# Moving one more product in six units to GpSimd, one more mask to ScalarE, and turning the weights later in a fused top-k attention and mixture-of-experts kernel

## Chip, core and metric

The kernel runs on one core of a Trainium2 chip. The metric is device time in microseconds (us) of one execution. The kernel before takes 995.38 us, the median of three runs (995.27 to 997.89). The engines are written as in the profile: PE is TensorE, PEld its weight loads, DVE is VectorE, ACT is ScalarE, POOL is GpSimd, and SP is the queue that issues the transfers.

## What is computed

There are two stages. The first is attention over 8 batches, 8 heads, 576 positions and head size 64, in which every row keeps only its 32 largest scores. The second routes the 4608 resulting rows of 512 to 8 experts, each of which takes at most 80 rows.

```python
def _attn_ref(q, k, v):
    scores = scale * np.matmul(q, k.transpose(0, 1, 3, 2))
    kth = np.partition(scores, -top_k, axis=-1)[..., -top_k:-top_k + 1]     # top_k = 32
    mask = scores >= kth
    scores = np.where(mask, scores, -1000000000.0)
    scores = scores - np.max(scores, axis=-1, keepdims=True)
    attn = np.exp(scores)
    attn = attn / (np.sum(attn, axis=-1, keepdims=True) + 1e-09)
    return np.matmul(attn, v).astype(np.float32)

def _moe_ref(x, w_gate, w1, w2, capacity):       # capacity = 80
    logits = x @ w_gate
    expert_idx = np.argmax(logits, axis=1)
    # ... softmax over the 8 logits; gate_w is that of the expert chosen
    out = np.zeros((N, D), dtype=np.float32)
    for e in range(E):
        # ... tok_idx: rows of expert e, cut to the 80 largest gate_w
        h = np.maximum(x[tok_idx] @ w1[e], 0.0)
        out[tok_idx] = gate_w[tok_idx, None] * (h @ w2[e])
    return out
```

## The kernel before

The attention works on one pair of heads at a time. There are 32 pairs. A pair has five tiles of rows: four full ones of 128 rows of each of the two heads, and a last one with the remaining 64 rows of both heads. A "unit" is 128 rows with their 576 scores, so a full tile has two units, the last tile has one, a pair has nine, and the kernel has 288.

All engines are programmed by hand as a pipeline. In each step, one unit enters. Its search for the 32nd largest score runs over five steps, interleaved on VectorE with the searches of earlier units. The letters in the strings below are the pieces of that search. "G" is one of six maxima over 96 scores. "a" to "e" are the top-8 maxima and replacements among the 48 candidates, and "e" also starts ScalarE's sign of the scores against the 24th largest, whose sum counts them. "y" is the product of scores and signs, "g" the top-8 of that product, "h" the pick of the threshold, and "m" the mask of the scores below it. "z" is a reciprocal.

```python
def search(self, i):
    ...                                     # "a" to "e": maxima and replacements on VectorE
            nc.scalar.activation(sign, s, Act.Sign, bias=w9[:, 7:8], scale=-1.0, accum_out=cnt)
    ...
    y = self.rows.tile([P, S], F32, name="y", tag="y", bufs=1)
    engine = nc.gpsimd if i in self.odd else nc.vector
    engine.tensor_tensor(out=y, in0=s, in1=sign, op=Alu.mult)                      # "y"
    yield
    nc.vector.max(out=w9[:, 8:], in_=y)                                            # "g"
    yield
    ...
    nc.vector.scalar_tensor_tensor(out=pick, in0=past, scalar=cnt, in1=w9[:, 7:],
                                   accum_out=self.thr[:, i : i + 1], ...)          # "h"

def below(self, i):                                                                # "m"
    self.mask[i] = self.rows.tile([P, S], BF16, name="mask", tag="mask", bufs=3)
    if i in self.odd:
        nc.scalar.activation(self.mask[i], self.s[i], Act.Relu, bias=self.thr[:, i : i + 1], scale=-1.0)
        return
    nc.gpsimd.tensor_scalar(self.mask[i], self.s[i], self.thr[:, i : i + 1], None, op0=Alu.is_lt)
```

`self.odd` holds every second unit. Those have the product on GpSimd and the mask on ScalarE; the others have the product on VectorE and the mask on GpSimd.

When both units of a tile have their masks, TensorE turns the scores so that keys lie on partitions. The turned mask, times a large negative number, is accumulated on top, and ScalarE takes the exponential out of PSUM. Each head's 576 keys are cut into five chunks of 128, the last of which overlaps the fourth, so a full tile has ten chunks.

```python
def turn_w(self, n, t):
    ...
    for h in range(g):                       # scores: 5 chunks of each head
        for c in range(NK):
            nc.tensor.matmul(dst[h][c], lhsT=sc[:, keys[c]], rhs=ident, ..., is_transpose=True)
    for h in range(g):                       # masks: the same chunks
        for c in (NF, *range(NF)):
            nc.tensor.matmul(dst[h][c], lhsT=mk[:, keys[c]], rhs=huge if i + h in self.odd else minus, ...)
    nc.scalar.activation(wT[:, 2 * NF : 2 * NF + g, :]..., cc[:, : g * P], Act.Exp, ...)     # last chunks
    nc.scalar.activation(wT[:, : g * NF, :], ab..., Act.Exp, ...)                            # the other eight
```

The rest of a step, in program order, where `i` is the step:

```python
for c in "ghmGbGycGdGGGeaz" if i % 2 else "GbGhmgcGdGeGGyaz":   # y of unit i-2, g of i-3, h and m of i-4
    ...
if rest: back()                              # weights times values, unit i-5 (the last tile of a pair)
if whole(i - 4): self.turn_w(*units[i - 4][:2])
for u in done: self.divide(*u)               # ScalarE: xn = weighted sum / sum of weights
if busy: self.front(*units[f][:2])           # scores of a tile that enters four steps on; ScalarE: s
if not rest: back()
if due and not busy: self.turn(due.pop())    # q and k of the next pair turned; ScalarE: both
for g in list(later): ...                    # norm: xn turned, ScalarE: xT; then gate logits, ScalarE: part
```

`front`, `turn`, and the two parts of `norm` all use one PSUM buffer, `sp`, of four banks. So each of them on TensorE waits until ScalarE has emptied the one before. The turned weights have one buffer `ab` of their own.

After the attention, `finish` routes the rows and computes the experts. Weights of experts 0 to 3 are loaded during the attention, those of expert 4 when the attention's memory is released, and the others into buffers that earlier experts leave.

Of the kernel before, what the change touches and what calls it, by code (L numbers as in the profile page):

```python
# [22 lines left out]
HUGE = 2.0 ** 100  # L23
# [4 lines left out]
def kernel(  # L28
# [120 lines left out]
    class Attention:  # L149


        def __init__(self, stack, lean):
            self.lean = lean
            pool = lambda name, bufs, **kw: stack.enter_context(tc.tile_pool(name=name, bufs=bufs, **kw))
            self.nat, self.qkp, self.rows = pool("nat", 1), pool("qkp", 2), pool("rows", 2)
            self.small, vpool = pool("small", 4), pool("vpool", 1)
            self.ps_s, self.ps_w, self.ps_c = (pool(n, k, space=PSUM) for n, k in (("ps_s", 1), ("ps_w", 1), ("ps_c", 2)))
            self.qk, self.turned, self.lg = {}, {}, {}
            self.s, self.top, self.cnt, self.y, self.mask, self.w, self.xn = ({} for _ in range(7))
            self.thr, self.z = thr_all, z_all  # L160
            self.odd = set()


            self.vb = []
            for j in range(1 if lean else 3):
                t = vpool.tile([P, NK, 2, D + 1], F32, name=f"vb{j}")
                nc.gpsimd.memset(t[:, :, :, D : D + 1], 1.0)
                nc.gpsimd.memset(t[: P - TL, NF, :, :], 0.0)
                self.vb.append(t)

            self.xT = vpool.tile([P, NK * P], F32, name="xT")
            nc.gpsimd.memset(self.xT[:, S:], 0.0)

        def load(self, n, b, hp):
            one = bass.ds(b, 1)
            tiles = []
            for name, src in (("qn", q), ("kn", k)):
# [7 lines left out]
                tiles.append(t)  # L185
            t = self.vb[n % len(self.vb)]
            for h in range(2):
                nc.sync.dma_start(
                    t[:, :NF, h, :D], v[one, 2 * hp + h, : NF * P, :].rearrange("o (c p) d -> p (o c) d", p=P))
            nc.sync.dma_start(  # L190
                t[P - TL :, NF, :, :D], v[one, 2 * hp : 2 * hp + 2, NF * P :, :].rearrange("o h p d -> p (o h) d"))
            self.qk[n] = tiles
# [23 lines left out]
        def front(self, n, t):  # L216
# [11 lines left out]
            s = self.rows.tile([P, 2 * S], F32, name="s", tag="s", bufs=2 if self.lean else 5)  # L228
# [43 lines left out]

        def below(self, i):

            self.top.pop(i)
            self.mask[i] = self.rows.tile([P, S], BF16, name="mask", tag="mask", bufs=3)
            if i in self.odd:
                nc.scalar.activation(self.mask[i], self.s[i], Act.Relu, bias=self.thr[:, i : i + 1], scale=-1.0)  # L278
                return
            nc.gpsimd.tensor_scalar(self.mask[i], self.s[i], self.thr[:, i : i + 1], None, op0=Alu.is_lt)  # L280
# [13 lines left out]
        def drop(self, i):  # L294

            s, top = self.s[i], self.top.pop(i)
            self.mask[i] = self.rows.tile([P, S], BF16, name="mask", tag="mask", bufs=2)
            nc.vector.tensor_scalar(self.mask[i], s, self.thr[:, i : i + 1], top[:, 0, 0:1], op0=Alu.is_lt, op1=Alu.add)

        def turn_w(self, n, t):  # L300
# [9 lines left out]
            keys = [slice(c * P, c * P + P) for c in range(NF)] + [slice(S - P, S)]  # L310
            dst = [[ab[:, h, c, :] for c in range(NF)] + [cc[:, h * P : (h + 1) * P]] for h in range(g)]

            for h in range(g):
                sc = self.s.pop(i + h)
                for c in range(NK):
                    nc.tensor.matmul(dst[h][c], lhsT=sc[:, keys[c]], rhs=ident, start=c == 0 or (c == NF and h == 0), stop=False,  # L316
                                     is_transpose=True, skip_group_check=True)
            for h in range(g):
                mk = self.mask.pop(i + h)
                for c in (NF, *range(NF)):  # L320
                    nc.tensor.matmul(dst[h][c], lhsT=mk[:, keys[c]], rhs=huge if i + h in self.odd else minus, start=False, stop=True, skip_group_check=True)  # L321
            wT = self.rows.tile([P, 2 * NK, P], F32, name="wT", tag="wT")
            nc.scalar.activation(wT[:, 2 * NF : 2 * NF + g, :].rearrange("p h r -> p (h r)"), cc[:, : g * P], Act.Exp,  # L323
                                 scale=scale / TINY)
# [3 lines left out]
        def back(self, n, t):  # L328
# [3 lines left out]
            for h in range(2 if t < NF else 1):  # L332
                o = slice(2 * P + h * (D + 1), 2 * P + (h + 1) * (D + 1))
                for c in range(NK):
                    for r in range(0, P, TL):
                        nc.tensor.matmul(cc[r : r + TL, o], lhsT=wT[:, h * NF + c if c < NF else 2 * NF + h, r : r + TL],  # L336
                                         rhs=vb[:, c, h if t < NF else r // TL, :], start=(c == 0), stop=(c == NF))
            self.w[n, t] = cc

        def over(self, n, t):  # L340
# [3 lines left out]
            sums = self.w[n, t][:, 2 * P : 2 * P + 2 * (D + 1)].rearrange("p (h d) -> p h d", h=2)[:, :g, D]  # L344
# [5 lines left out]
        def divide(self, n, t):  # L350
# [3 lines left out]
            for h in range(2):  # L354
                if t < NF:
                    p, o, j, m = slice(0, P), 2 * P + h * (D + 1), h, P
                else:
                    p, o, j, m = slice(TL * h, TL * h + TL), 2 * P, 0, TL
                nc.scalar.activation(self.xn[n][:m, t, h, :], cc[p, o : o + D], Act.Copy, scale=self.z[p, n % NP, t, j : j + 1])  # L359

        def norm(self, n, b, hp, bi, nb, cs=range(NK)):
# [15 lines left out]
            yield 1  # L377
# [50 lines left out]
        def run(self, slow):  # L428
# [6 lines left out]
            self.odd = set(range(1, NU, 2))  # L435
# [10 lines left out]
            def step(i, last):  # L446
                if 0 <= i < NU:
                    n, t, h = units[i]
                    if t == 2 and h == 1 and n + 2 < NP:
                        self.load(n + 2, *divmod(n + 2, HP))  # L450
                    if t in (1, 3) and h == 0 and slow and n:
# [5 lines left out]
                back = dict(a=0, b=1, c=1, d=1, e=1, y=2, g=3, h=4, m=4)  # L457

                for c in "ghmGbGycGdGGGeaz" if i % 2 else "GbGhmgcGdGeGGyaz":
# [11 lines left out]
                    elif c == "m":  # L471
                        if 0 <= i - back[c] < NU:
                            self.below(i - back[c])
                    elif i - back[c] in second:
                        next(second[i - back[c]])
# [3 lines left out]
                def back():  # L479
                    if whole(i - 5):  # L480
                        self.back(*units[i - 5][:2])
                        drawn.append(units[i - 5][:2])


                rest = whole(i - 4) and units[i - 4][2] == 2
                if rest:
                    back()
                if whole(i - 4):
                    self.turn_w(*units[i - 4][:2])
# [15 lines left out]
                for g in list(later):  # L505
                    if ready[g] and busy and not last:
# [10 lines left out]
            with tc.manual_schedule():  # L517
                self.load(0, 0, 0)
                self.load(1, *divmod(1, HP))
# [3 lines left out]
                while i < NU + 6 or later:  # L523
                    step(i, i >= NU + 5)
# [3 lines left out]
        def batch(self, b):  # L528

            for hp in range(HP):  # L530
                self.load(hp, b, hp)
                self.turn(hp)
# [200 lines left out]
    def finish(wpool, full):  # L733

        stack = ctx.enter_context(ExitStack())
        late = stack.enter_context(tc.tile_pool(name="late", bufs=1))
        for dma in load_w(4, late):
            dma()
# [124 lines left out]
    with ExitStack() as main:  # L863
        wpool = main.enter_context(tc.tile_pool(name="wpool", bufs=4))
        for e in range(4):
# [5 lines left out]
    with tc.If(nc.values_load(bad[0:1, 0:1]) > 0):  # L871
# [6 lines left out]
        with ExitStack() as again:  # L878
            wpool = again.enter_context(tc.tile_pool(name="wpool2", bufs=4))
            for e in range(4):  # L880
# [34 lines left out]
```

## Time and profile before

The profiled execution spans 993.1 us. The attention fills it up to about 870 us; routing and experts take the rest.

| what | value |
|---|---|
| busy over the whole span | PE 885.5 us, DVE 870.6, ACT 797.2, POOL 451.9 |
| busy from 100 to 800 us, as shares | DVE 99%, ACT 93%, PE 91%, POOL 51% |
| product of one unit on VectorE / on GpSimd | 747 ns / 1283 ns |
| mask of one unit on ScalarE / on GpSimd | 780 ns / 1723 ns |
| transfers | 85.76 MB, 86 GB/s on average |

Busy time counts instructions that overlap only once. Consecutive instructions of one engine overlap by some tens of ns, so the distance from one start to the next (here "pitch") is shorter than the duration, and work is added up by pitch. The idle time that the profile gives stands before an instruction, with the engine whose result ended it.

### The profile page before, as it was taken

What the parts mean: (1) busy time and instruction counts of PE and PEld (TensorE: products, weight loads), DVE (VectorE), ACT (ScalarE), POOL (GpSimd) and SP (SyncE); (2) the same over time, 40 slices, a digit from 0 to 9 for tenths busy, and PEclk for the clock granted to TensorE, in tenths of its full rate; (3) what the DMA queues carried; (4) which work ended last, traced back from release to release, by engine and by line L of the source; (5) the groups of instructions that cost most, each with busy time, mean ns of one, the idle gap of its engine ahead of it and who ended that gap; (6) DMA issues with size and microseconds to landing.
All of it is one profiled execution on the core that took longest, in us unless ns stands there. A gap on an engine that the chain in (4) does not pass through costs nothing.

```text
span 993.1 us, 35590 instructions
## 1 busy us (share of the span) xinstructions
PE 885.5 (89%) x13368; PEld 704.9 (71%) x13368; DVE 870.6 (88%) x5072; ACT 797.2 (80%) x1652; POOL 451.9 (46%) x330
## 2 busy tenths in 40 slices
PE   5899999998989989899899999999899898679996
PEld 3677777776767777677677777777677676668896
DVE  5899999999999999999999999999999999571110
ACT  3899999999999989999999999999899999601110
POOL 2445555555455545554555555555455555302111
PEclk9999999999999999999999999999999999979998
DMA  3344453333332323333333322222222100044920
GB/s 72 97 126 131 129 134 92 92 92 92 91 79 62 87 82 86 92 92 93 88 82 83 91 49 51 50 50 50 50 50 49 41 23 14 16 170 142 382 76 28
DMA packets 167893, 85.76 MB, mean 86 GB/s; under 512 B 117792, under 2 KB 154656, under 8 KB 167712
## 3 DMA queue, kind: packets, MB, share of 16 engines
q1 hardware_dynamic: 166688, 80.78, 29.7%
q0 software_dynamic: 1024, 2.62, 0.9%
q8 instruction: 107, 1.75, 0.7%
q14 instruction: 74, 0.61, 0.2%
HBM read 63.19 MB, written 20.19 MB: 84 GB/s over the span
## 4 chain that ended last, share of the span: by engine, by line
DVE 53%; PE 24%; ACT 18%; issue 5%; DMA 1%; POOL 0%; POOLq 0%; SPq 0%; ACTq 0%; DVEq 0%
DVE cand L241 17%; DVE w L266 12%; DVE cand L260 6%; DVE y L264 6%; ACT s L233 4%; DVE top L252 4%; PE yp L799 4%; ACT wT L325 3%; PE sp L201 3%; PE cc L336 3%; ACT sign L257 3%; DVE pick L269 3%; ACT mask L278 2%; PE sp L226 2%; PE ab L316 2%
## 5 line engine op out<-in xcount | busy, mean ns | idle before, releaser
L241 DVE MAX8 cand<-s 128x8 f32<-128x96 f32 x1728 | 393.9, 250 | 8.9 <-ACT s L233 8.8
L280 POOL TENSOR_SCALAR mask<-s,thr_all 128x576 bf16<-128x576 f32 x144 | 248.2, 1723 | 144.9 <-DVE pick L269 121.8
L264 POOL TENSOR_TENSOR y<-s,sign 128x576 f32<-128x576 f32 x144 | 184.8, 1283 | 277.3 <-DVE pick L269 128.0
L336 PEld LDWEIGHTS cc<-vb,wT 128*64 128x64 f32 x5760 | 181.7, 138 | 111.2 <-ACT wT L325 98.5
L257 ACT ACTIVATE sign<-s,w 128x576 bf16<-128x576 f32 x288 | 225.4, 783 | 22.8 <-DVE w L252 22.2
L336 PE MATMUL cc<-vb,wT 128*64 128x65 f32 x5760 | 204.0, 225 | 40.6 <-ACT wT L325 38.9
L266 DVE MAX8 w<-y 128x8 f32<-128x576 f32 x288 | 217.8, 756 | 2.5 <-POOL y L264 2.5
L226 PE MATMUL sp<-both 64*128 64x288 f32 (+1 forms) x1280 | 202.1, 435 | 15.0 <-ACT part L388 6.5
L233 ACT ACTIVATE s<-sp 128x1152 f32<-128x1152 f32 (+1 forms) x161 | 167.3, 1040 | 12.7 <-PE sp L226 11.9
L316 PE MATMUL ab<-ident,s 128*128 128x128 f32 x1148 | 175.6, 282 | 0.0
L325 ACT ACTIVATE wT<-ab 128x1024 f32<-128x1024 f32 (+1 forms) x159 | 148.8, 936 | 0.0
L226 PEld LDWEIGHTS sp<-both 64*128 64x128 f32 (+1 forms) x1280 | 105.6, 179 | 53.8 <-ACT part L388 8.5
L316 PEld LDWEIGHTS ab<-ident,s 128*128 128x128 f32 x1148 | 127.5, 141 | 11.6 <-issue 0.9
L321 PEld LDWEIGHTS <-mask 128*128 128x128 bf16 x1440 | 92.1, 98 | 42.4 <-ACT mask L278 19.6
L252 DVE MAX8 top<-cand 128x8 f32<-128x48 f32 x576 | 116.9, 203 | 0.0
L260 DVE MATCH_REPLACE8 cand<-top,cand 128x48 f32<-128x48 f32 x576 | 112.9, 196 | 0.0
L278 ACT ACTIVATE mask<-s,thr_all 128x576 bf16<-128x576 f32 x144 | 112.3, 780 | 0.4
L264 DVE TENSOR_TENSOR y<-s,sign 128x576 f32<-128x576 f32 x144 | 107.6, 747 | 4.5 <-ACT sign L257 4.5
L359 ACT ACTIVATE xn<-cc,z_all 128x64 f32<-128x64 f32 (+1 forms) x320 | 86.5, 318 | 1.4 <-DVE z_all L348 0.8
L316 PE MATMUL cc<-ident,s 128*128 128x128 f32 x288 | 78.9, 274 | 0.3 <-ACT xn L359 0.2
L269 DVE SCALAR_TENSOR_TENSOR pick<-past,cnt,w 128x9 f32<-128x9 f32 x288 | 69.5, 241 | 0.2 <-DVE z_all L348 0.2
L323 ACT ACTIVATE wT<-cc 128x256 f32<-128x256 f32 (+1 forms) x160 | 56.2, 351 | 12.0 <-PE cc L321 11.3
(188 smaller groups left out, 965.7 us busy)
## 6 DMA issues: line engine op xcount, KB each, us to landing
w<-in_moe_w_dram SPq DMA_DIRECT2D x32, 512.0 KB, 4.7
w<-in_moe_w_dram SPq DMA_DIRECT2D x8, 2048.0 KB, 9.8
out_dram<-zero SPq DMA_DIRECT2D x9, 1024.0 KB, 6.3
qn<-in_q_dram SPq DMA_DIRECT2D x64, 128.0 KB, 2.6
kn<-in_k_dram SPq DMA_DIRECT2D x64, 128.0 KB, 2.5
vb<-in_v_dram SPq DMA_DIRECT2D x64, 128.0 KB, 2.6
xd<-xn SPq DMA_DIRECT2D x32, 256.0 KB, 4.3
qn<-in_q_dram SPq DMA_DIRECT2D x32, 32.0 KB, 2.5
```

Source lines behind the costliest of these rows:

```text
L226: nc.tensor.matmul(o, lhsT=qT[d, t * P : t * P + m], rhs=kT[d, j * HS : (j + 1) * HS], start=True, stop=True)
L233: nc.scalar.activation(s[:, j * HS : (j + w) * HS].rearrange("p (j c) -> p j c", c=HS), ps[:, j : j + w, :HS], Act.Copy, scale=TINY)
L241: nc.vector.max(out=cand[:, j, :], in_=s[:, j * S // NG : (j + 1) * S // NG])
L252: nc.vector.max(out=dst, in_=cand)
L257: nc.scalar.activation(sign, s, Act.Sign, bias=w9[:, 7:8], scale=-1.0, accum_out=cnt)
L260: nc.vector.match_replace(out=cand, in_to_replace=dst, in_values=cand, imm_value=LOW)
L264: engine.tensor_tensor(out=y, in0=s, in1=sign, op=Alu.mult)
L266: nc.vector.max(out=w9[:, 8:], in_=y)
L280: nc.gpsimd.tensor_scalar(self.mask[i], self.s[i], self.thr[:, i : i + 1], None, op0=Alu.is_lt)
L316: nc.tensor.matmul(dst[h][c], lhsT=sc[:, keys[c]], rhs=ident, start=c == 0 or (c == NF and h == 0), stop=False, is_transpose=True, skip_gr ...
L325: nc.scalar.activation(wT[:, : g * NF, :], ab.rearrange("p h c r -> p (h c) r")[:, : g * NF, :], Act.Exp, scale=scale / TINY)
L336: nc.tensor.matmul(cc[r : r + TL, o], lhsT=wT[:, h * NF + c if c < NF else 2 * NF + h, r : r + TL], rhs=vb[:, c, h if t < NF else r // TL, ...
```

## The change

- **Who does what.** Two of three units, instead of one of two, have the product on GpSimd and the mask on ScalarE. Of 288 units that is 192 instead of 144. The order of the pieces within a step goes by threes to match.
- **Later masks.** The masks that GpSimd makes are issued one step later, at i-5. The product and mask of different units then need not follow each other so tightly.
- **Weights turned two steps later.** `turn_w` is at i-6 and `back` at i-7, so that masks are finished when TensorE comes to them. This takes more buffers for scores (seven tiles for five) and masks; in exchange only three experts' weights are loaded early, and those of expert 3 come with expert 4's.
- **Nine chunks.** The two heads' scores of a full tile lie side by side in 1152 columns, which are cut into nine chunks of 128. The middle chunk holds 64 keys of each head. Values are laid out to match, with zeros at the other head's keys. That takes one more load of values for each pair.
- **Gate logits** are computed inside `turn_w`, between scores and masks, instead of in a slot of their own.

```diff
-            self.odd = set(range(1, NU, 2))
+            self.odd = set(i for i in range(NU) if i % 3 < 2)
...
-                for c in "ghmGbGycGdGGGeaz" if i % 2 else "GbGhmgcGdGeGGyaz":
+                for c in "GbGhmgcGdGeGGyaz" if i % 3 == 1 else "ghmGbGycGdGGGeaz":
...
-                        if 0 <= i - back[c] < NU:
-                            self.below(i - back[c])
+                        for k in (4, 5):
+                            if 0 <= i - k < NU and (i - k in self.odd) == (k == 4):
+                                self.below(i - k)
...
-                    if whole(i - 5):
+                    if whole(i - 7):
...
-                if whole(i - 4):
-                    self.turn_w(*units[i - 4][:2])
+                def gate():
+                    for g in later:
+                        if ready[g] == 2:
+                            ready[g] = next(g)
+                if whole(i - 6):
+                    self.turn_w(*units[i - 6][:2], gate)
... in turn_w
-            keys = [slice(c * P, c * P + P) for c in range(NF)] + [slice(S - P, S)]
+            keys = [slice(c * P, c * P + P) for c in range(2 * NF + 1)] if t < NF else ...
-            nc.scalar.activation(wT[:, 2 * NF : 2 * NF + g, :].rearrange("p h r -> p (h r)"), cc[:, : g * P], Act.Exp,
-                                 scale=scale / TINY)
+            nc.scalar.activation(wT[:, 2 * NF, :], cc[:, :P], Act.Exp, scale=scale / TINY)
... in front
-            s = self.rows.tile([P, 2 * S], F32, name="s", tag="s", bufs=2 if self.lean else 5)
+            s = self.rows.tile([P, 2 * S], F32, name="s", tag="s", bufs=2 if self.lean else 7)
... in load_v
+            for j, h, k0 in ((0, 0, 0), (1, 1, TL), (2, 1, 0)):
+                nc.sync.dma_start(t[:, j * NF : (j + 1) * NF, :D], v[one, 2 * hp + h, k0 : k0 + NF * P, :]...)
... in finish
-        late = stack.enter_context(tc.tile_pool(name="late", bufs=1))
-        for dma in load_w(4, late):
-            dma()
+        late = stack.enter_context(tc.tile_pool(name="late", bufs=2))
+        for e in (3, 4):
+            for dma in load_w(e, late):
+                dma()
```

## The prediction

> **What bounds the kernel now.** I read the busy table first, then the attention alone (from 50 to 850 us), then the groups of instructions, the chain that ended last, and ScalarE's timeline over two pairs of heads. The busy table names no winner, so I asked for the attention alone; the columns are PE, PEld, DVE, ACT and POOL.
>
> ```profile
> 50.00:850.00 800.00, 728.36 (x10506) 569.96 (x10502) 795.25 (x4732) 744.28 (x1544) 411.96 (x274) 1.00 0.30 77
> ```
>
> VectorE is busy 99% of this stretch, ScalarE 93%, TensorE 91%. Taken alone this says that VectorE is the bound and that a product taken off it is pure gain. The chain says otherwise. In some pairs it runs through VectorE alone; in this one, from 515 us, it runs through TensorE and ScalarE for 20 us and then returns to VectorE:
>
> ```profile
> 516.69 1.39 PE cc L336 x40
> 518.12 1.66 PE sp L201 x10
> 519.80 0.47 ACT both L214
> ...
> 534.80 0.20 ACT sign L257
> 535.02 0.76 DVE y L264
> 535.97 0.66 DVE w L266
> ```
>
> The reader is to see that two chains of nearly the same length share the loop. The pitch of the loop shows on ScalarE's `xT` copy, one per pair: it starts at 513.34, 539.65 and 565.60 us, so a pair takes 26.31 and 25.95 us, 26.13 us on average. Which chain leads changes from one pair to the next, because nine units are odd and the work alternates by twos.
>
> The pieces that the change moves are these groups (count, then busy us and mean ns, then idle before them):
>
> ```profile
> L280 POOL TENSOR_SCALAR mask<-s,thr_all 128x576 bf16<-128x576 f32 x144 | 248.2, 1723 | 144.9 <-DVE pick L269 121.8
> L264 POOL TENSOR_TENSOR y<-s,sign 128x576 f32<-128x576 f32 x144 | 184.8, 1283 | 277.3 <-DVE pick L269 128.0
> L278 ACT ACTIVATE mask<-s,thr_all 128x576 bf16<-128x576 f32 x144 | 112.3, 780 | 0.4
> L264 DVE TENSOR_TENSOR y<-s,sign 128x576 f32<-128x576 f32 x144 | 107.6, 747 | 4.5 <-ACT sign L257 4.5
> ```
>
> And this is ScalarE in a stretch where it never waits but for `both`:
>
> ```profile
> 541.33 0.36 ACT L323 ACTIVATE wT<-cc 128x256 f32<-128x256 f32 x1
> 541.60 1.01 ACT L325 ACTIVATE wT<-ab 128x1024 f32<-128x1024 f32 x1
> 542.50 0.52 ACT L359 ACTIVATE xn<-cc,z_all 128x64 f32<-128x64 f32 x2
> 542.89 1.15 ACT L233 ACTIVATE s<-sp 128x1152 f32<-128x1152 f32 x1
> 543.90 0.80 ACT L278 ACTIVATE mask<-s,thr_all 128x576 bf16<-128x576 f32 x1
> 544.57 0.80 ACT L257 ACTIVATE sign<-s,w 128x576 bf16<-128x576 f32 x1
> 545.24 0.22 ACT L257 ACTIVATION_READ_ACCUMULATOR sign<-s,w 128x1 f32 x1
> 545.78 1.13 ACT L214 COPY both<-sp 128x1152 f32<-128x1152 f32 x1 [0.32 <-PE sp L201]
> ```
>
> From start to start, a mask costs ScalarE 0.67 us (544.57 less 543.90), not its 0.78 us of duration.
>
> **What the Trainium skill says.** "ScalarE: Activation LUTs", section "What ACT_TABLE_LOAD costs", says that activations back to back overlap by about 93 ns. The trace agrees: 0.78 against 0.67 us. "GPSIMD Engine Reference", section "4.1 Engine selection", says that two-input work on GpSimd takes about twice VectorE's time and one-input work is roughly at line rate. The product agrees loosely (1283 against 747 ns, 1.7 times); the one-input mask does not, at 1723 ns. So the swap of a mask for a product relieves GpSimd. The same page, section "8. Key points", has GpSimd contend with VectorE instructions that read two SBUF inputs. The trace agrees: `pick`, a two-input instruction, has a median of 214 ns but reaches 1286 ns, as long as one GpSimd product.
>
> **The change, part by part, for one pair (nine units).**
>
> *VectorE.* It goes from 4.5 products to 3. A product costs it 0.66 us from start to start (one starts at 511.27 us, the next instruction at 511.93), so 1.5 x 0.66 = 0.99 us leaves. Where VectorE leads the chain (113.70 to 136.62 us, eight steps), a step takes 2.865 us, so nine take 25.8 us. After: **24.8 us**. Over 32 pairs this is 32 us, the gain if VectorE were the only bound.
>
> *ScalarE.* Its work in a pair, by pitches of the trace: nine signs with their sums, 9 x 0.77 = 6.93; 4.5 masks, 3.02; exponentials of four full tiles at 0.27 + 0.90 and of the last at 0.64, 5.32; `xn` 4 x 0.40 + 0.65 = 2.25; `s` 4 x 1.01 + 0.55 = 4.59; `both`, `xT` and `part` 1.63. The sum is 23.74 us, so of 26.13 us it waits or idles 2.39. The change adds 1.5 masks, 1.00 us. Nine chunks shorten the first exponential from 256 columns to 128. By duration this saves 79 ns (367 less 288), by pitch about 0.11 us (0.27 less 0.16 in a last tile at 551.57 us), so 0.44 us a pair. After: 23.74 + 1.00 - 0.44 = **24.30 us** of work, before any wait.
>
> *TensorE.* A full tile loses one fp32 transpose (pitch 0.11 us) and one mask product (0.055 to 0.07 us), 0.18 us, or 0.7 us a pair. TensorE stays near 90% of the pair.
>
> *Waits on masks.* With weights turned two steps later, masks are ready. What goes is TensorE's wait for masks, 19.1 + 18.8 us on its weight loads in 800 us, and through them ScalarE's wait for the first exponential, 6.4 us, 0.2 us a pair. This matters little by itself: TensorE's waiting is mostly covered by the next wait.
>
> *Waits that stay.* They come from the single buffer `sp`, and here I worked through a pair by hand, step by step, in the changed order. (1) `both` starts 1.88 us after `s` gives the engine free (545.78 less 543.90), since TensorE needs 1.66 us for ten transposes. Between them the new order has one mask and one sign, 1.44 us; ScalarE waits 0.44. (2) `xT` starts 1.09 us after `s` (565.60 less 564.51) with only a sign between, 0.77; it waits 0.32. (3) In the steps around the last tile, TensorE now has, with no gap: the turn of `xn` 0.79, a full tile's turn 1.04, gate logits 0.73, masks 0.64, scores of the last tile 1.12, weights times values 1.31, the last tile's turn 0.97, scores of the next pair 1.24: 7.84 us. From 0.9 us into it, ScalarE has `xT` 0.53, masks 1.34, signs 1.54, `part` 0.07, exponentials 1.70, `xn` 0.40 and `s` 0.55: 6.13 us. It waits 7.84 - 0.90 + 0.05 - 6.13 = 0.86. Together 1.6 us.
>
> *Sum.* ScalarE's loop with TensorE is 24.30 + 1.62 = **25.9 us** a pair. It exceeds VectorE's 24.8, so it sets the pace: 26.13 - 25.92 = 0.21 us a pair, times 31 pairs is 6.5 us. This is my chosen reading: most of VectorE's 32 us turns into VectorE waiting for late signs.
>
> *Ends.* At the end of the attention one more tile is still to be turned when VectorE finishes, and the last unit's mask is on GpSimd (1.72 us) instead of ScalarE; most lies in gaps of the drain. I take +1 us. The extra 4 MB of expert weights follow at the release of memory. Expert 4's 4 MB land between about 869 and 882 us at some 350 GB/s, so 8 MB end near 894; the first gather of rows starts at 896 us. I take 0, with a microsecond of risk. The extra value load adds 4 MB over the loop, where DMA is 30% busy: 0. So 995.4 - 6.5 + 1 = 990; the ScalarE pitches are from saturated stretches and a few hundredths on each side pull towards gain, so I say **989 us**.
>
> **Rivals.** *VectorE is the bound and everything else fits:* 24.8 us a pair plus perhaps 0.3 of coupling, so 26.13 to 25.1, about 32 us less, 963 to 968 us. For it speak VectorE's 99% and 53% of the chain; against it that ScalarE would have to work 24.3 of 25.1 us when three waits on `sp` alone take 1.6. *ScalarE's extra masks cost more than is saved:* if the shorter exponential saves only its 79 ns and the waits stay at today's 2.39 us, ScalarE's loop is 24.42 + 2.39 = 26.8 us, 21 us more, 1017 us. Against it: part of today's waits are VectorE's (21.4 us in 800 on the top-8 `w`, 0.7 us a pair) and go when ScalarE is behind. *GpSimd products block VectorE:* 48 more of them, each able to hold a `pick` for up to 1.28 us. `pick` averages 241 ns against 214 now, 8 us in all. By thirds, the pick that follows closely on a GpSimd product comes in one step of three, not one of two, so I expect this to shrink slightly; were it to double, it would cost 8 us, and only if VectorE led.
>
> **Range and chances.** Each 0.1 us in a pair is 3.2 us. My sum of waits may be off by 0.3 us a pair and the pitches by 0.15, some 11 us either way; the first rival is the far lower tail. So 974 to 1000. Faster by over 2% means below 975.5, a gain of 0.65 us a pair, of which I have found 0.2: 0.13. Slower by over 2% needs the second rival nearly whole: 0.03. Within 2%: 0.84.
>
> **What would show it.** Right: VectorE's busy share in the loop falls to about 96%, with new idle time before `y` or `w`, released by ScalarE's sign or GpSimd's `y`; ScalarE rises to 95% or more, with its idle before `both`, `xT` and `s`, released by TensorE; ScalarE's wait on `w` all but gone; waits for masks gone on TensorE; 96 VectorE products. The chain would show more of ACT and PE than 53% DVE leaves now. Wrong: VectorE still at 99%, or ScalarE with idle below 1 us a pair, or an `s` of the next pair's first tile that does not wait.

## The result, and the profile after

The changed kernel takes **1006.31 us** (1006.11 to 1007.94), where the kernel before, timed beside it, takes 996.48 (995.27 to 997.89): a ratio of 1.010, 95% interval 1.008 to 1.012. It is 1% slower. 989 us were predicted, with 1000 as the upper end of the range.

First the busy table and the chain that ended last, from the page of the changed kernel, and then the attention alone (from 50 to 850 us; columns PE, PEld, DVE, ACT, POOL, the granted clock, the share of DMA and GB/s).

```profile
PE 865.9 (86%) x13112; PEld 689.4 (69%) x13112; DVE 874.5 (87%) x5024; ACT 810.3 (81%) x1700; POOL 428.4 (43%) x333
...
DVE 70%; PE 18%; ACT 7%; issue 3%; POOL 1%; DMA 1%; POOLq 0%; SPq 0%; DVEq 0%; ACTq 0%
```

```profile
50.00:850.00 800.00, 703.89 (x10204) 551.78 (x10198) 794.77 (x4647) 751.23 (x1576) 385.76 (x272) 0.99 0.30 77
```

VectorE gave away a third of its products, but its chain share rose from 53 to 70% and it still reads 99% busy. The groups of the same stretch say what its busy time holds now:

```profile
L273 POOL TENSOR_TENSOR y<-s,sign 128x576 f32<-128x576 f32 x181 | 231.5, 1279 | 413.2 <-ACT sign L266 185.3 <-DVE cand L250 80.5 <-DVE pick L278 66.8
...
L294 ACT ACTIVATE mask<-s,thr_all 128x576 bf16<-128x576 f32 x182 | 142.2, 781 | 0.7
...
L278 DVE SCALAR_TENSOR_TENSOR pick<-past,cnt,w 128x9 f32<-128x9 f32 x273 | 90.9, 333 | 0.0
...
L273 DVE TENSOR_TENSOR y<-s,sign 128x576 f32<-128x576 f32 x91 | 67.7, 744 | 1.2 <-ACT sign L266 1.0
```

The products went where they were meant to go. But `pick`, a small instruction, takes 333 ns on average (330 over the whole run, where it was 241 before). The timeline of a long one, with GpSimd and ScalarE beside it:

```profile
515.26 0.76 ACT L266 ACTIVATE sign<-s,w 128x576 bf16<-128x576 f32 x1
...
516.18 1.27 POOL L273 TENSOR_TENSOR y<-s,sign 128x576 f32<-128x576 f32 x1 [3.02 <-DVE cand L250]
...
516.39 1.10 DVE L278 SCALAR_TENSOR_TENSOR pick<-past,cnt,w 128x9 f32<-128x9 f32 x1
...
517.49 0.76 DVE L275 MAX8 w<-y 128x8 f32<-128x576 f32 x1
```

`pick` starts under GpSimd's product and ends as that product ends. VectorE is counted busy, though it only stands: in an ordinary pair the nine `pick` stand 1.1 us beyond 214 ns each. The next instruction, the top-8 of `y`, needs that very product, and the product started late because ScalarE's sign came late: that sign, the first line, ends at 516.02. The profile names VectorE's `cand` as what ended the product's wait, but 175 of the 181 products of the stretch start within 0.25 us of the end of a sign, whatever it names. So the 99% hide a wait for ScalarE.

ScalarE's own waits in the stretch (total, count, longest):

```profile
ACT s L242 <- PE sp L234: 17.8, 31, 0.6
ACT both L222 <- PE sp L209: 13.9, 29, 2.4
ACT sign L266 <- DVE w L261: 6.2, 6, 1.7
ACT xT L397 <- PE sp L209: 5.7, 29, 0.2
```

Idle in all, it is 48.8 of the 800 us, 1.6 us a pair, and 37.4 us of that are waits for TensorE on `sp`. The wait on VectorE's `w`, 21.4 us over 48 times before, has shrunk to 6.2.

**Where the 11.4 us are** (spans of 1004.5 and 993.1 us). I split them at three marks: the first copy `both` within the loop (at 25.60 and 25.19 us), the last one, and the last write of routing values `R`. The start takes 0.4 us more, the 30 pairs between the two copies 4.3 (787.57 against 783.27), the drain to `R` 3.9 (67.5 against 63.6), routing and experts 2.8 (123.9 against 121.1). Within the loop, the distance between copies shows two kinds of pairs. An ordinary pair takes 26.09 us, one like the other, where before they alternated between 25.98 and 26.18 to 26.29. But each of the three pairs in which gates are computed takes 29.2 to 30.1 us (27.2 before), and the one after the third 27.0.

### The profile page after: what moved, and what is told of

Its sections match the earlier page's. It is cut to its first block, busy times and chain, and to the rows that moved or that the text cites. A ratio compares the mean times of both kernels' runs of the same rounds, so it can differ in the third digit from the quotient of the medians.

```text
span 1004.5 us, 35059 instructions
## 1 busy us (share of the span) xinstructions
PE 865.9 (86%) x13112; PEld 689.4 (69%) x13112; DVE 874.5 (87%) x5024; ACT 810.3 (81%) x1700; POOL 428.4 (43%) x333
## 4 chain that ended last, share of the span: by engine, by line
DVE 70%; PE 18%; ACT 7%; issue 3%; POOL 1%; DMA 1%; POOLq 0%; SPq 0%; DVEq 0%; ACTq 0%
DVE cand L250 23%; DVE w L275 16%; DVE cand L269 9%; DVE pick L278 6%; DVE y L273 5%; DVE top L261 5%; PE yp L832 4%; PE cc L357 3%; DVE w L261 2%; ACT sign L266 2%; PE sp L209 2%; ACT wT L344 2%; PE sp L234 2%; DVE z_all L369 2%; PE ab L334 1%
## 5 line engine op out<-in xcount | busy, mean ns | idle before, releaser
L273 POOL TENSOR_TENSOR y<-s,sign 128x576 f32<-128x576 f32 x192 | 245.6, 1279 | 449.6 <-ACT sign L266 210.4
L250 DVE MAX8 cand<-s 128x8 f32<-128x96 f32 x1728 | 385.3, 246 | 9.1 <-ACT s L242 9.1
L357 PE MATMUL cc<-vb,wT 128*64 128x65 f32 x5760 | 207.4, 227 | 70.8 <-ACT wT L344 69.0
L296 POOL TENSOR_SCALAR mask<-s,thr_all 128x576 bf16<-128x576 f32 x96 | 165.3, 1722 | 2.1 <-DVE pick L278 2.1
L294 ACT ACTIVATE mask<-s,thr_all 128x576 bf16<-128x576 f32 x192 | 149.9, 782 | 0.7
L278 DVE SCALAR_TENSOR_TENSOR pick<-past,cnt,w 128x9 f32<-128x9 f32 x288 | 95.1, 330 | 0.0
L340 PE MATMUL ab<-huge,mask 128*128 128x128 bf16 x1148 | 90.5, 220 | 0.0
L340 PEld LDWEIGHTS <-mask 128*128 128x128 bf16 x1312 | 84.6, 98 | 2.2
L334 PE MATMUL cc<-ident,s 128*128 128x128 f32 x160 | 45.5, 284 | 33.0 <-ACT xn L380 33.0
L273 DVE TENSOR_TENSOR y<-s,sign 128x576 f32<-128x576 f32 x96 | 71.4, 744 | 1.7 <-ACT sign L266 1.4
```

Of the source, the lines that this page charges most:

```text
L250: nc.vector.max(out=cand[:, j, :], in_=s[:, j * S // NG : (j + 1) * S // NG])
L334: nc.tensor.matmul(o, lhsT=sc[:, keys[c]], rhs=ident, start=c in (0, NF, NF + 1), stop=False, is_transpose=True, skip_group_check=True)
L340: nc.tensor.matmul(dst[c], lhsT=mk[:, keys[c]], rhs=minus if self.lean else huge, start=False, stop=True, skip_group_check=True)
```

## Experiments

### The parts apart

Two theories stood after the result. One kept to the prediction: ScalarE with TensorE sets the pace, and the assignment of two in three loads ScalarE too much. The other: more GpSimd products hold VectorE up at `pick`.

**e1: the changed kernel with the units halved again.**

```diff
-            self.odd = set(i for i in range(NU) if i % 3 < 2)
+            self.odd = set(range(1, NU, 2))
-                for c in "GbGhmgcGdGeGGyaz" if i % 3 == 1 else "ghmGbGycGdGGGeaz":
+                for c in "ghmGbGycGdGGGeaz" if i % 2 else "GbGhmgcGdGeGGyaz":
```

> The changed kernel with its assignment undone: every second unit has the product on GpSimd and the mask on ScalarE again, in the old order by twos; nine chunks, later turning, later GpSimd masks and late expert weights stay. Theory A (ScalarE with TensorE sets the pace of the changed loop, 24.8 us of work and 1.6 us of waits a pair): ScalarE loses 1.0 us a pair and falls to about 25.4, below VectorE's 25.8, so a pair takes about 25.9 us instead of 26.4, some 15 us less than the changed kernel: 989 to 994 us, and VectorE leads. Theory B (GpSimd's products blocking the pick, a two-input VectorE instruction, are the cause): VectorE gets 31 us of products back and loses some 25 us of blocking, so 1006 to 1012 us.

Measured: 1016.25 us, ratio 1.019 (1.017 to 1.022). Both expectations fell. Without the new assignment the rest of the change is worse, not better.

**e2: in the changed kernel, the top-8 of `y` ahead of `pick` in one step of three.**

```diff
-                for c in "GbGhmgcGdGeGGyaz" if i % 3 == 1 else "ghmGbGycGdGGGeaz":
+                for c in "GbGghmcGdGeGGyaz" if i % 3 == 1 else "ghmGbGycGdGGGeaz":
```

> The changed kernel with two letters swapped in one step of three: the top-8 of the product (g), which has to wait for GpSimd's product anyway, goes ahead of the pick (h), so that no pick can run beside that product. Mean pick back to about 215 ns in both theories. Theory A: the wait only moves from the pick to g, as VectorE idle time released by GpSimd; 1002 to 1007 us. Theory B: the 25 us of blocking are gone; 980 to 985 us.

Measured: 1005.72 us, ratio 1.009 (1.007 to 1.012), the changed kernel's time. The groups and VectorE's waits from 50 to 850 us:

```profile
L278 DVE SCALAR_TENSOR_TENSOR pick<-past,cnt,w 128x9 f32<-128x9 f32 x273 | 58.3, 214 | 0.0
```

```profile
DVE w L275 <- POOL y L273: 35.4, 55, 1.0
```

`pick` is back at 214 ns, and what it had stood is now an open wait, 35.4 us, for GpSimd's product. The contention is real, as "GPSIMD Engine Reference", section "8. Key points", in the Trainium skill says of instructions with two SBUF inputs, but it cost nothing here.

**e3: the last tile's weights times values after the turn, not ahead of it** (`rest = whole(i - 6) and ...` becomes `rest = False`).

> The changed kernel with weights times values of the tile before the last put behind the last tile's turn and the next pair's scores, in the one step of nine where it ran ahead of them. It takes 1.3 us of TensorE out of the way of one s copy of ScalarE, which waits 0.6 us a pair. Theory A: up to 0.6 us a pair less, so 988 to 998 us. Theory B: no change, 1003 to 1007 us.

Measured: 1030.71 us, ratio 1.035 (1.032 to 1.038). The wait on `s` is gone, but VectorE now waits for its reciprocal's input:

```profile
DVE z_all L369 <- PE cc L357: 28.9, 29, 1.3
```

This run did two things at once: it took the products of values out of the way of `s`, and it made them late for the reciprocal. So it says nothing for or against the stretch. It does show that VectorE's reciprocal stands in line, and that a late product of values holds up the searches behind it.

**e4: the kernel before with the new assignment alone** (the two lines of e1, the other way round).

> The kernel before with the assignment alone changed: two of three units with GpSimd's product and ScalarE's mask, order by threes; ten chunks, turning at i-4, everything else as before. Theory A: ScalarE's work grows by 1.0 us a pair to 25.4 without the shorter exponential or the earlier-ready masks, and with its 1.6 us or more of waits a pair takes 27 us or more: 1010 to 1030 us. Theory B: much as the changed kernel's loop, 990 to 1003 us.

Measured: 1038.57 us, ratio 1.042 (1.039 to 1.044). With everything else as before, the assignment costs 42 us; with the rest of the change it brings 10 (1016.25 to 1006.31). So something in the rest makes the assignment usable. The later masks and the later turn are the likely parts; no run tells them from each other or from the nine chunks.

**e5: the kernel before with only three experts' weights early** (`wpool` of 3, expert 3 in `late`).

> The kernel before with one part of the change alone: three experts' weights loaded during the attention instead of four, those of expert 3 with expert 4's when the attention's memory is released. My prediction counted 0 us for it, with a microsecond of risk. If the 2.8 us by which routing and experts are longer in the changed kernel come from these 4 MB: 998 to 1000 us. If they come from elsewhere: 995 to 997 us.

Measured: 998.16 us, ratio 1.002 (1.001 to 1.003), against 996.2 of before: 2 us.

**e6: nine chunks and late weights, all else but the buffers as before.** Made from the changed kernel with units halved as in e1, masks at `i - 4`, the turn at `i - 4`, `back` at `i - 5`, and the logits in a slot of their own:

```diff
-            yield 2
+            yield 1
-                if whole(i - 6):
-                    self.turn_w(*units[i - 6][:2], gate)
+                if whole(i - 4):
+                    self.turn_w(*units[i - 4][:2])
```

> The changed kernel with the old assignment and the old times of masks, turning and gate logits (masks at i-4, weights turned at i-4, weighted sum at i-5, logits in a slot of their own): nine chunks remain, and the late weights of expert 3. Theory A (ScalarE with TensorE sets the pace): 0.4 us a pair less on ScalarE and 0.7 on TensorE in the pairs that these led, so 988 to 994 us with the late weights' 1 to 3 us in it, and the loss of the run with the assignment undone (1016 us) is that of the later turning. If nine chunks themselves cost: 1000 us or more.

Measured: **993.64 us**, ratio 0.997 (0.996 to 0.998), pairs of 25.93 us on average. Against e5 the nine chunks bring 4.5 us. This part alone is better than both kernels.

**e7 and e8: more work on ScalarE, more on VectorE.** Both start from the changed kernel. In e7 the first head's `xn` is written twice, in e8 one maximum in two of three units is taken twice.

```diff
-                nc.scalar.activation(self.xn[n][:m, t, h, :], ...)
+                for _ in range(2 - h):
+                    nc.scalar.activation(self.xn[n][:m, t, h, :], ...)
```

```diff
-                nc.vector.max(out=cand[:, j, :], ...)
+                for _ in range(2 if j == 3 and i % 3 else 1):
+                    nc.vector.max(out=cand[:, j, :], ...)
```

> The changed kernel with one more ScalarE instruction in each tile: the normalising copy of the first head is done twice, with the same result, about 0.2 us by pitch, 1.0 us a pair. Theory A: ScalarE sets the pace, so all of it appears, 28 to 36 us: 1034 to 1042 us. Theory C (VectorE, by its chain of products, sets the pace): 1006 to 1015 us.

> The changed kernel with one more VectorE instruction in two of three units: one of the maxima over 96 scores is done twice, with the same result, 0.16 us by pitch, 1.0 us a pair. Theory A: VectorE's 0.9 us a pair of waiting takes most of it: 1006 to 1015 us. Theory C: all appears, 1034 to 1040 us.

Measured: 1048.61 us with ordinary pairs of 27.47 (e7; ratio 1.053, 1.049 to 1.056), and 1043.29 with 27.09 (e8; ratio 1.047, 1.043 to 1.050). By pitch, `xn` takes 1.76 us a pair more in e7 (3.99 against 2.23), of which 1.38 came out; ScalarE's wait on `s` took up 0.32. In e8, 0.98 were added and 1.00 came out. So most of the one and all of the other came out, and they didn't tell which engine leads. In e8 ScalarE waits again (in all, and in one ordinary pair):

```profile
ACT sign L267 <- DVE w L262: 24.5, 31, 2.2
```

```profile
703.37 0.78 ACT L267 ACTIVATE sign<-s,w 128x576 bf16<-128x576 f32 x1 [0.88 <-DVE w L262]
```

### The later turn

The remaining step, from e6 to e1, cost 22.6 us. I suspected that the lags pile up TensorE's work: by the order of the program, the last tile's turn now falls in the same step as the next pair's first scores.

**e9: e1 with the gate logits in their own slot** (`yield 2` becomes `yield 1`), so e6 with the change's lags (GpSimd's masks at `i - 5` among them).

> The lags of the change (weights turned six steps after their search, multiplied seven after) with units halved as before and the gate logits in their own step, as in the kernel before; so against the nine-chunks kernel (993.6 us) only the lags differ, and against the half-assignment kernel (1016.3 us) only the place of the logits. Theory 'the lags pile TensorE's work up': the last tile's turn now lies in the same step as the scores of the next pair, wherever the logits are, so 1013 to 1020 us and TensorE still waits about 1.3 us a pair for xn before that turn. Rival 'the logits inside the turn make it': 994 to 1003 us, and the wait on xn below 0.5 us a pair.

Measured: 1007.93 us, ratio 1.012 (1.010 to 1.013). Between the two: the lags cost 14.3 us, the logits inside the turn another 8.3. In e1's trace TensorE's clock is halved seven times from 60 to 850 us, in e9's never, so a part of the 8.3 may be the clock. ScalarE's waits in e9:

```profile
ACT both L222 <- PE sp L209: 18.5, 29, 1.0
ACT s L242 <- PE sp L234: 16.9, 30, 0.6
```

In e6 `both` has 18.6 us and `s` does not appear. So the new wait is `s`, 0.55 us a pair, in the stretch that the prediction named; the time of an ordinary pair rose by some 0.35 us (26.3 against 25.93). In the traces the loop takes 9.6 us more and the drain 3.2.

**e10: e6 with the turn one step later, not two** (`turn_w` at `i - 5`, `back` at `i - 6`).

> The nine-chunks kernel (993.6 us) with weights turned one step later rather than two (lags five and six). Turns then fall in steps 6, 8, 1, 3 and 4 of a pair's nine, scores in 5, 7, 0, 2 and 4: no full tile's turn shares a step with scores, and the last tile's turn no longer meets the next pair's scores. Theory 'piling up': 988 to 996 us, no steady pairs above 26.1 us, TensorE's waits for masks gone. Rival 'each step of delay costs by itself' (buffers come free later, the end drains later): halfway between 993.6 and 1016.3, 1003 to 1007 us.

Measured: 1038.73 us, ratio 1.044 (1.039 to 1.048). Both expectations fell. TensorE's and VectorE's waits:

```profile
PE sp L234 <- ACT xT L397: 64.5, 29, 3.2
PE sp L234 <- ACT both L222: 35.2, 29, 1.3
```

```profile
DVE z_all L369 <- PE cc L357: 31.5, 45, 1.8
```

At one step the turn leaves the steps that have scores, and the products of values enter them. They stand behind the scores, which wait for `sp`, and VectorE's reciprocal waits for them. The steps alternate, and of the delays that were run (none, one, two) the odd one breaks the alternation. My reading by "piling up" counted work per step and missed who stands behind whom.

**e12: e10 with the assignment by threes and all masks at `i - 4`** (the lines of e1, the other way round).

> As the kernel with lags five and six, and GpSimd's product with ScalarE's mask in two of three units as in the change, all masks made four steps after. Theory 'the assignment pays once the masks have a step of room and TensorE's work is not piled up': 0.3 to 0.5 us a pair below the half-assignment kernel with the same lags, 975 to 985 us. Rival 'ScalarE is the bound, and 1.5 masks more in a pair cost it 1.0 us': 15 to 31 us above that kernel.

Measured: 1128.54 us, ratio 1.132 (1.129 to 1.135): 90 us above e10, against 15 to 31 by the rival. The same wait of VectorE has more than tripled, and the granted clock was 0.91 over the run (0.98 in e10). TensorE now idles 2.57 us in nearly every pair, and nearly every time its clock is halved afterwards, mostly for 6.83 us; in e10 that happened five times from 60 to 850 us.

```profile
DVE z_all L369 <- PE cc L357: 104.2, 76, 2.6
```

How much of the wait's growth comes from the halved clock I didn't follow up.

### The three long pairs

In a pair with a gate, VectorE also does the gate's small instructions, up to three to a step. The timeline of one, in the changed kernel:

```profile
273.63 0.24 DVE L437 TENSOR_REDUCE gw<-el 128x10 f32<-128x80 f32 x1 [0.21 <-ACT el L428]
273.90 0.17 DVE L438 TENSOR_SCALAR gw<-gw 128x10 f32<-128x10 f32 x1
...
274.11 0.22 DVE L439 RECIPROCAL gw<-gw 128x10 f32<-128x10 f32 x1
...
274.24 0.70 DVE L275 MAX8 w<-y 128x8 f32<-128x576 f32 x1
...
276.42 0.20 DVE L261 MAX8 w<-cand 128x8 f32<-128x48 f32 x1
...
276.72 0.77 ACT L266 ACTIVATE sign<-s,w 128x576 bf16<-128x576 f32 x1 [1.69 <-DVE w L261]
```

The bunch makes `w` late and ScalarE stands 1.69 us before a sign. TensorE then stands too, 2.82 us at each of the three gates, and each time its clock falls afterwards (the column after POOL): for 3.41 us at the first two gates, for 10.24 at the third.

```profile
278.60:281.90 3.30, 3.19 (x44) 2.96 (x44) 3.30 (x20) 2.90 (x7) 0.32 (x1) 0.50 0.01 2
490.20:493.50 3.30, 2.77 (x42) 2.65 (x43) 3.30 (x17) 3.30 (x7) 0.00 (x0) 0.50 0.00 0
700.00:703.00 3.00, 0.26 (x4) 0.26 (x6) 3.00 (x21) 2.26 (x7) 2.10 (x2) 0.80 0.01 3
703.00:706.00 3.00, 3.00 (x44) 2.70 (x42) 3.00 (x17) 2.53 (x5) 0.39 (x1) 0.50 0.02 5
706.00:712.00 6.00, 6.00 (x32) 4.75 (x32) 4.31 (x32) 3.74 (x7) 2.37 (x3) 0.50 0.43 98
```

"TensorE: Matmul & The Clock Gate", section "HAM oscillation — how this bites in real kernels", in the Trainium skill gives gaps over about 3.4 us as what brings the clock down; here an idle stretch that the profile gives as 2.82 us preceded each fall.

The trace of e2 tells what the clock costs. It has the same three idle stretches (2.83 us) and the same ordinary pairs (26.10 us), but only the second was followed by a fall:

```profile
274.00:286.00 12.00, 8.17 (x124) 6.19 (x121) 12.00 (x79) 9.99 (x21) 6.76 (x5) 1.00 0.37 98
485.00:497.00 12.00, 8.26 (x98) 6.49 (x98) 11.03 (x72) 8.95 (x19) 5.71 (x5) 0.86 0.22 51
697.00:709.00 12.00, 8.16 (x124) 6.20 (x120) 12.00 (x79) 9.99 (x21) 6.74 (x5) 1.00 0.22 51
```

Its pairs with gates take 28.07, 29.26 and 28.09 us. So the bunch itself costs some 2.0 us, and a fall of 3.41 us another 1.2. In the changed kernel the three pairs and the one after the third take 11.4 us more than ordinary ones; measured against e2's 28.1, some 5.4 of these are the clock's.

**e11: the changed kernel with the gate's VectorE instructions spread, one to a step but for one pair of small ones** (a `yield 0` between those that shared a step; the first of them below).

```diff
             nc.vector.tensor_reduce(mx, lg, axis=AX, op=Alu.max)
+            yield 0
             nc.vector.tensor_tensor(out=lg, in0=lg, in1=mx..., op=Alu.subtract)
```

> The changed kernel, the gate's VectorE instructions one to a step rather than up to three, over eleven steps rather than four. Theory 'the three pairs with gates lose 3 to 4 us each because a bunch of VectorE work makes a sign late and TensorE then idles': the pairs fall from about 29.3 to 27.2 us and the time from 1006.3 to 999 to 1002 us. Rival 'they lose time to the clock that is granted or to the transfers beside them': 1005 to 1007 us, pairs still over 29 us.

Measured: 998.80 us, ratio 1.0024 (1.0014 to 1.0034), 7.5 us below the changed kernel. Pairs with gates take 26.3 to 27.1 us, two after another; ordinary ones are unchanged at 26.10. TensorE's longest idle stretch in the loop is now 1.79 us, and its clock isn't halved there. From 690 to 702 us it is 1.00:

```profile
690.00:702.00 12.00, 10.85 (x150) 8.58 (x150) 12.00 (x75) 11.62 (x25) 5.55 (x4) 1.00 0.34 83
```

**e15: e6 with the same spreading.**

> The nine-chunks kernel (993.6 us), its gates spread over eleven steps. If a bunch of VectorE work at the gates costs it as it costs the changed kernel, three pairs lose 0.5 to 1 us less each: 990 to 992.5 us. If only lags of six and seven are sensitive to it: 993 to 995 us.

Measured: 992.03 us, ratio 0.995 (0.994 to 0.997): 1.6 us below e6. That is little against the spread of both, but the traces agree: a pair with a gate and the next one together take 53.04 us, where they take 53.48 in e6, 1.3 us over the three. The bunch costs both orders something, and the changed one some five times as much.

### Who sets the ordinary pair

**e13: e11, with the first maximum of a unit over 16 columns instead of 96.** The keys in 80 columns are left out of the search.

```diff
+                w = S // NG if j else 16
-                nc.vector.max(out=cand[:, j, :], in_=s[:, j * S // NG : (j + 1) * S // NG])
+                nc.vector.max(out=cand[:, j, :], in_=s[:, j * S // NG : j * S // NG + w])
```

> The changed kernel with its gates spread (998.8 us, pairs of 26.10 us), and the first of a unit's six maxima over 16 columns rather than 96 (so the top keys of 80 columns are left out of the search): VectorE loses about 0.7 us a pair, nothing else changes. Theory 'ScalarE with TensorE sets the pace, VectorE has 1 us of slack' (the prediction's): 997 to 999.5 us, pairs of 26.05 to 26.10. Theory 'VectorE sets the pace': 976 to 982 us, pairs of 25.4 us. Theory 'the two share it, each leading in a part of the pair': between, 985 to 993 us.

Measured: 3476.23 us, ratio 3.49 (3.48 to 3.49). I had overlooked that the kernel counts whether its candidates sufficed and otherwise does the batches again by a slow exact search, and with the columns left out it does. The total is useless, but the first pass over the pairs is whole. Its line, after that of e11:

```profile
50.00:850.00 800.00, 702.58 (x10288) 550.45 (x10285) 799.40 (x4702) 758.25 (x1592) 390.55 (x276) 1.00 0.30 77
```

```profile
50.00:850.00 800.00, 702.95 (x10282) 550.58 (x10282) 772.32 (x4709) 759.48 (x1597) 393.06 (x277) 1.00 0.30 77
```

VectorE (third column) is 27 us less busy, and an ordinary pair takes 26.10 us as before, to the hundredth. In e13 VectorE stands idle for 1.17 us of it, before the top-8 of `y`. **VectorE does not set the pace.**

**e14: e11, with `xn` of both heads of a full tile in one ScalarE instruction**, by the first head's sum; the second head's own division is left out.

```diff
+            if t < NF:
+                two = cc[:, P : P + 2 * (D + 1)]...[:, :, :D]
+                nc.scalar.activation(self.xn[n][:, t, :, :], two, Act.Copy, scale=self.z[:, n % NP, t, 0:1])
+                return
```

> The changed kernel with its gates spread, and both heads' weighted values of a full tile scaled in one instruction by the first head's sum (so the second head's division is left out): ScalarE loses about 0.5 to 0.6 us a pair. Theory 'ScalarE with TensorE sets the pace': all of it comes off, 980 to 984 us, pairs of 25.55 us. Theory 'VectorE sets the pace': 997 to 999.5 us. Theory 'they share it': between, 987 to 993 us.

Measured: 990.98 us, ratio 0.995 (0.993 to 0.996), pairs of 25.74. By pitch `xn` lost 0.57 us a pair (1.57 to 1.00), and 0.36 came off. Nearly all of the rest came back as ScalarE's waits for TensorE: in an ordinary pair 0.12 us at the first exponential of the last tile, 0.04 at `both` and 0.03 at `xT`. The last two also show in the sums over 800 us, of e11 and then of e14:

```profile
ACT both L222 <- PE sp L209: 9.3, 29, 0.3
ACT xT L397 <- PE sp L209: 5.7, 29, 0.2
```

```profile
ACT both L222 <- PE sp L209: 10.4, 29, 0.4
ACT xT L401 <- PE sp L209: 6.8, 29, 0.2
```

So ScalarE leads at 26.10, with TensorE close behind it. How near VectorE's own limit lies, these two runs don't show.

**e16: e11 with the logits in their own slot** (`yield 2` becomes `yield 1`).

> The changed kernel with its gates spread, and the gate logits in their own step rather than inside a tile's turn. In the half assignment this gave 8 us back. If the logits inside the turn lengthen TensorE's stretch at the end of a pair here too: 991 to 996 us, pairs of 25.9 us; if that stretch is not what sets the pace: 998 to 1001 us, pairs of 26.1 us.

Measured: **991.95 us**, ratio 0.996 (0.995 to 0.997), pairs of 25.87: 0.23 us a pair less than e11, 6.9 us. ScalarE's row that differs between the two is the first exponentials, 1.05 us a pair by pitch in e11 and 0.84 here; with the logits between scores and masks, the second exponential's input comes later. This is the whole change with two small repairs, and it is faster than the kernel before, level with e15.

## Why the prediction was wrong, point by point

The path that sets the pace was predicted rightly. Three terms of the sum failed: ScalarE's work in an ordinary pair was taken 0.69 us too small (24.30 predicted, 24.99 measured; 5.3 us in the loop after smaller waits), the pairs with gates were left out (some 5.5 us), and the ends were taken as +1 us and came as +7.1.

By single steps, the kernels form a row: before 996.2, late weights 998.2 (e5), nine chunks 993.6 (e6), lags 1007.9 (e9), logits in the turn 1016.3 (e1), assignment 1006.3 (after). Each difference holds for this order only; e4 shows how differently the assignment counts elsewhere.

- **"ScalarE+TensorE sets the pace": right** for ordinary pairs (e13, e14). The waits are the three that were named, though smaller: in an ordinary pair (from 547.19 us) `both` waits 0.32, `xT` 0.20 and `s` 0.58 us, together 1.10 where 0.44 + 0.32 + 0.86 = 1.62 were predicted.
- **The size of ScalarE's work: the step that failed in ordinary pairs.** 25.92 us were predicted and 26.09 came, 5.3 us over 31 pairs. From start to start, ScalarE's instructions of that pair add up to 24.99 us, with the short gaps that the profile doesn't name, where 24.30 were predicted; the waits fall short by 0.52, and 0.17 remain. The term furthest off is the exponentials, 5.32 - 0.44 = 4.88: they take 5.29 (1.05 the first ones, 3.64 the second ones of full tiles, 0.60 that of the last tile). The 0.44 rested on a first exponential of 0.16 us, but five take 0.21 on average, and 0.17 only without the logits in the turn (e16: 0.84 for five). I had put the logits into TensorE's stretch alone. The last tile's second one takes 0.60, and 0.48 were reckoned. Signs (7.09 for 6.93) and `s` (4.73 for 4.59) make up most of the rest.
- **Three pairs with gates: left out.** The sum counted 31 equal pairs. VectorE had slack in an ordinary pair, but in a pair with a gate a bunch of its work, in the wrong step, went through `w` and the sign to TensorE, and TensorE's idle stretch brought half a clock. The loop took 4.3 us more instead of 6.5 less, a miss of 10.8 us: 5.3 of it lie in ordinary pairs, so some 5.5 in these three and the one after. Spreading them gives back 7.5 (e11), more than the change had lost there, since the kernel before lost some too (27.2 us against about 26.1 in its ordinary pairs).
- **Ends: +1 us predicted, +7.1 measured.** The late weights, taken as 0, cost 2 us (e5). The drain takes 3.9 more, and this goes with the lags: from the last `both` to the last `R` it is 63.6 us in e6 and 66.8 in e9, which differ in the lags alone. The last exponentials start at 865.01, 869.15 and 872.85 us with waits of 2.32 and 1.88 us for TensorE between (2.04 and 1.22 before), so one more tile to turn was not hidden. That the weights are what makes routing and experts 2.8 us longer fits e5's trace (125.1 us against 121.1) but is not shown for each part: in e4, whose weights come as before, they take 123.2.
- **Rival "GpSimd products block VectorE":** I expected it to shrink, and `pick` grew by 25 us in all (95.1 against 69.5). It had no effect (e2).
- **"This matters little by itself", of the masks that no longer wait:** I treated the two steps of delay as free but for the stretch. In the half assignment the delay cost 14 us (e9). With the new assignment, all the rest of the change together brings 32 us (e4 to the changed kernel); how much of that is the delay, no run shows.
- **VectorE's share:** expected to fall to 96%, it stayed at 99%, which I had named as a mark of being wrong. It wasn't one: the share contained the standing `pick`. Without it VectorE's own work in an ordinary pair is 25.0 us (26.09 less 1.1), close to the 24.8 predicted.

Why an addition of 0.98 us to VectorE comes out whole (e8), though taking work away changes nothing (e13), I explain by its place: it makes `w` late for the sign. An ordinary pair of e8 has one wait that the changed kernel doesn't have, 0.88 us for `w`, which is most of the 1.00. That speaks for it; no run moved the addition elsewhere. How much of e8 is TensorE's clock (0.963 over the run) stays open.

## What to carry to other kernels

Split a change into its parts and run them one after another: here two of them brought something (nine chunks, assignment), three cost more, and only the sum was seen. Count the rare iterations apart from the ordinary ones; work that fits on average can still be late in one step, and what follows down the chain multiplies it. A busy share near 100% proves a bound only if less work on that engine shortens the loop.

## What the runs showed of the hardware

- A two-input VectorE instruction with a median of 213 ns took up to 1.2 us under a GpSimd product (1.28 us) and was counted busy all that time; the profile shows no wait.
- After each of three idle stretches of 2.82 us, TensorE was granted half its clock, for 3.41, 3.41 and 10.24 us. In e2 only one of three such stretches was followed by that, for 3.41 us. In e12, with 2.57 us idle in nearly every pair, the clock over the whole run was 0.91.
